# A third landing tile for the weights' double words, and fewer tile shapes: one attention + spectral + FFN kernel

## The chip, the cores and the metric

The kernel runs on one core of one Trainium2 chip. The time is device microseconds of one execution, as the median of several; the profile is that of one execution, taken on the same core, and its times start at the first instruction. Engines are named as in the profile: PE is TensorE, PEld its weight loads, DVE VectorE, ACT ScalarE, POOL GpSimd, SP the engine whose queue issues every DMA here.

## The reference, cut to what matters

Eight batches, twelve heads, 448 tokens, 64 numbers a head. Queries and keys are normalized, attention gives `x` of 448 x 768 per batch; a two-dimensional Fourier transform is mixed in, and a feed-forward block (FFN) of 768 x 3072 x 768 follows. The FFN's two weight matrices come as 64-bit floats.

```
attn = softmax(scale * rmsnorm(q, g_q) @ rmsnorm(k, g_k).T) @ v
u  = x + real(fft(fft(x, axis=1), axis=2))
un = (u - mean(u)) / sqrt(var(u) + 1e-06)
out = u + relu(un @ w_ch1) @ w_ch2        # w_ch1, w_ch2: float64
```

## The kernel before, in words

**Two streams of work.** For each batch `b`, `aux(b)` yields the attention of six pairs of heads (`attention`), then the transform and the residual rows (`spectral`); `ffn(b)` yields the feed-forward block: 24 steps `up(m)`, each 18 matmuls from a piece `w1` of 768 x 128, and 36 steps `down(g, d)`, each 12 matmuls from a piece `w2` of 512 x 128 (with one `up` ahead, four `up`, six `down`, and so on). `merge` interleaves `ffn(b)` with `aux(b + 1)` by costs written in the yields and a ratio (`RATIO_FIRST` for batch 0, `RATIO` after). The first batch's `aux(0)` has no FFN beside it and runs alone, with 28 steps of `aux(1)` mixed into its end.

**Weights.** The matmuls take each weight as a rounded part and a remainder in fp32r. In batch 0 each of the 60 pieces is made from double words by `convert` (L659): a DMA brings the words as pairs of 32-bit halves into a tile `raw` (named `dbl...`, L664 to L667); ACT takes the magnitude of the high half into a tile `bits` (named `mag...`, L670) and scales the low half (L671); DVE clamps, shifts and joins (L672, L676, L680); POOL adds the low half (L684), ACT rounds (L685), POOL takes the remainder (L686); `converted` then stores both parts to device memory (L716), and later batches load them from there (L726). Fourteen of the 60 pieces are converted during `aux(0)` by `convert_some`; the other 46 while FFN 0 uses them, beside the attention of batch 1. The `dbl` tile is free again after L684, the `mag` tile after L686. There are two `dbl` tiles: `wide` gives the tag `X` 1800 words per partition, twice, and the same tag later holds the folded rows of batches 2 and up (`fold`). There are two `mag` tiles (`SLOTS["M"]`) and three weight tiles in each stream.

**A pair's rows.** `load_pair` (L214) issues four DMAs for the raw rows of queries and keys (112 partitions x 1024 words, tag `raw`, two tiles) and six for the values (128 x 512 words, tag `v`, two tiles), one pair ahead of use. `norm_pair` reads the rows and the values; in batch 0 the values go to PE as they are, and stay until `value_pair` is through.

**Order.** Tiles of one tag share a fixed number of slots: a tile waits until the tile that had its slot is read for the last time. A scheduler lays out the order of the instructions of each engine, the DMA queue on SP among them, when the program is built, and gives tiles addresses; tiles of different tags whose lives don't overlap may be given the same bytes, and then the later one waits for the earlier one's readers. At run time each engine goes through its list in order. The slots of all tags as written come to some 54,000 words (216 KB) per partition, the sum of all `bufs` times their sizes.

Of the kernel before, what the change touches and what calls it, by code (L numbers as in the profile page):

```python
# [11 lines left out]
F32 = mybir.dt.float32  # L12
F32R = mybir.dt.float32r
U32 = mybir.dt.uint32
# [5 lines left out]
B, H, S, D = 8, 12, 448, 64  # L20
DM = H * D
DFF = 4 * DM
C = 112
NC = S // C
NPAIR = H // 2
NR = DM // 128
# [63 lines left out]
def spectral_block(ctx, tc, q, k, v, g_q, g_k, w1, w2, d1, d2, out, nb=B):  # L90
# [4 lines left out]
    sb = ctx.enter_context(tc.tile_pool(name="sb", bufs=2))  # L95
# [32 lines left out]
    def behind(ins):  # L128

        others = given.get(ins.ins.engine, [])  # L130
        if starting[0] and len(others) > LAG:
            order(
                ins, others[-1 - LAG],
                mybir.DependencyClass.NoSync, mybir.DependencyReason.DATA,
            )
# [12 lines left out]
    def bank(tag, name):  # L148
        if tag == "either":
            tag = ("q", "av")[turn[0] % 2]  # L150
            turn[0] += 1
        return ps.tile([128, 512], F32, tag=tag, name=name, bufs=BANKS[tag])
# [6 lines left out]
    def wide(name, dtype=F32):  # L159
        return sb.tile([128, 1800], dtype, tag="X", name=name, bufs=2)  # L160

    def sub(o, a, b_):
        V.tensor_tensor(out=o, in0=a, in1=b_, op=ALU.subtract)
# [50 lines left out]
    def load_pair(b, p):  # L214
        if b >= nb or (b, p) in loaded:
            return
        raw = sb.tile([C, 2, 2, NC, D], F32, tag="raw", name=f"raw{b}_{p}")
        for i, src in enumerate((q, k)):
            for h in range(2):
                nc.sync.dma_start(  # L220
                    raw[:, i, h],
                    src[b, 2 * p + h].rearrange("(c t) d -> t c d", c=NC),
                )
        vt = sb.tile([128, 4, 2, D], F32, tag="v", name=f"v{b}_{p}")
        for h in range(2):
            nc.sync.dma_start(
                vt[:, :3, h],
                v[b, 2 * p + h, 64 * h : 64 * h + 384].rearrange(
                    "(j t) d -> t j d", t=128
                ),  # L230
            )
            for z in range(2):
                nc.sync.dma_start(
                    vt[64 * z : 64 * z + 64, 3, h],
                    v[b, 2 * p + h, 384 * (1 - h) : 384 * (1 - h) + 64],
                )
        loaded[b, p] = raw, vt

    def next_pair(b, p):
        return (b, p + 1) if p + 1 < NPAIR else (b + 1, 0)  # L240
# [43 lines left out]
    def plain_s(b, p):  # L284
        return b * NPAIR + p in PLAIN_SCORES
# [3 lines left out]
    def transpose_pair(b, p):  # L289

        if b >= nb or (b, p) in ready:
            return
        load_pair(b, p)
        qk, vhl = norm_pair(b, p)
        load_pair(*next_pair(b, p))
        yield 0

        if plain_s(b, p):
            T = []
            for i, tag in enumerate(("QT", "KD")):  # L300
                pt = bank(QK_BANKS[b > 0][i], f"qk{b}_{p}_{i}")
                for c in range(NC):
                    nc.tensor.transpose(
                        pt[:, c * C : (c + 1) * C],
                        qk[:, i, c].rearrange("t h d -> t (h d)"),
                        ident[:C, :C],
                    )
                t = sb.tile([128, S], F32, tag=tag, name=f"{tag}{b}_{p}")
                A.copy(t, pt[:, :S])
                T.append(t)  # L310
                yield 420
            ready[b, p] = T[0], T[1], vhl
            return

        QT = sb.tile([128, 2, S], F32R, tag="QT", name=f"QT{b}_{p}")
        KD = sb.tile([128, 2, S], F32R, tag="KD", name=f"KD{b}_{p}")
        for i in range(2):
            pt = bank(QK_BANKS[b > 0][i], f"qk{b}_{p}_{i}")
            for c in range(NC):
                nc.tensor.transpose(  # L320
                    pt[:, c * C : (c + 1) * C], qk[:, i, c].rearrange("t h d -> t (h d)"),
                    ident[:C, :C],
                )
            src = pt[:, :S]
            if i == 0:
                A.copy(QT[lo, 0], src[lo])
                A.copy(QT[hi, 1], src[hi])
                sub(QT[hi, 0], src[lo], QT[lo, 0])
                sub(QT[lo, 1], src[hi], QT[hi, 1])
            else:  # L330
                for h, sl in enumerate((lo, hi)):
                    A.copy(KD[sl, h], src[sl])
                    sub(KL[sl, h], src[sl], KD[sl, h])
                A.copy(KD[hi, 0], KD[lo, 0].bitcast(F32))
                A.copy(KD[lo, 1], KD[hi, 1].bitcast(F32))
            yield 420

        ready[b, p] = QT, KD, vhl

# [316 lines left out]
    w1w, w2w = w1.bitcast(U32), w2.bitcast(U32)  # L656
    kept1 = [dram.tile([128, 2, NR, 128], F32, name=f"w1_{m}") for m in range(NF)]
    kept2 = [dram.tile([128, NR, 2, 4, 128], F32, name=f"w2_{g}") for g in range(NG)]
    def convert(src, bits, part, name):  # L659

        _, c, f = src.shape
        raw = wide(f"dbl{name}", U32)[:, : c * f].rearrange(  # L664
            "r (c f w) -> r c f w", c=c, w=2
        )
        nc.sync.dma_start(raw.rearrange("r c f w -> r c (f w)"), src)  # L667
        low, high = raw[:, :, :, 0], raw[:, :, :, 1]
        value = bits.bitcast(F32)
        behind(nc.scalar.activation(value, high.bitcast(F32), AF.Abs))  # L670
        behind(nc.scalar.activation(low, low, AF.Copy, scale=2.0**-29))  # L671
        behind(nc.vector.tensor_scalar(  # L672
            out=value, in0=value, scalar1=MIN_HIGH, scalar2=MAX_HIGH,
            op0=ALU.max, op1=ALU.min,
        ))
        behind(nc.vector.tensor_scalar(  # L676
            out=bits, in0=bits, scalar1=5, scalar2=2,
            op0=ALU.logical_shift_left, op1=ALU.logical_shift_right,
        ))
        behind(nc.vector.scalar_tensor_tensor(  # L680
            out=bits, in0=high, scalar=0xC0000000, in1=bits,
            op0=ALU.bitwise_and, op1=ALU.bitwise_or,
        ))
        behind(nc.gpsimd.tensor_tensor(out=bits, in0=bits, in1=low, op=ALU.add))  # L684
        behind(nc.scalar.copy(part[0], value))  # L685
        behind(nc.gpsimd.tensor_tensor(  # L686
            out=part[1], in0=value, in1=part[0], op=ALU.subtract
        ))
# [46 lines left out]
            return self.parts.pop(0)  # L735

    def w1_doubles(m):
        return w1w[:, m * 256 : (m + 1) * 256].rearrange("(c r) f -> r c f", r=128)

    def w2_doubles(i):  # L740
        g, d = i // NR, i % NR
        return w2w[g * 512 : (g + 1) * 512, d * 256 : (d + 1) * 256].rearrange(
            "(f r) e -> r f e", r=128
        )

    def w2_kept(i):
        return kept2[i // NR][:, i % NR]
# [181 lines left out]

    load_gains()  # L930
    load_pair(0, 0)
    warm()
    second = aux(1)
# [20 lines left out]

# [19 lines left out]
```

## Time and profile before

| | |
|---|---|
| time, median of 3 runs | 2231.12 us (2231.12, 2231.13, 2229.54) |
| span of the profiled execution | 2227.2 us |
| PE busy | 2092.4 us, 94% |
| DVE busy | 1612.1 us, 72% |
| ACT busy | 1060.8 us, 48% |
| POOL busy | 536.6 us, 24% |
| mean granted TensorE clock | 0.970 |

The span goes from the first to the last instruction; the three runs have no spans of their own, and the median lies 3.9 us above the profiled span. Rows named `magw1e`, `dblw2e` and the like are those of the 14 early pieces, `magw` and `dblw` those of the 46 pieces that are converted during FFN 0; `w` is a weight tile. A wait "`X <- Y: a, n`" says that X's engine stood idle for `a` us, n times, until Y ended. The chain of waits is followed back from the last instruction, and its lines give start, length and what was being waited for or done.

### The profile page before, as it was taken

How to read it: one execution, taken by the hardware profiler on the slowest of the kernel's cores; microseconds unless marked ns; L12 is line 12 of the kernel's file. 1: busy time of each engine (PE TensorE's matmuls, PEld its weight loads, DVE VectorE, ACT ScalarE, POOL GpSimd, SP SyncE). 2: the span in 40 equal slices, each digit the busy share in tenths (PEclk: the TensorE clock that was granted, in tenths of full speed). 3: DMA queues.
4: the chain of work that ended last, by engine and by line, in shares of the span. 5: the costliest groups of instructions: out<-in, count | busy, mean ns of one | idle time of the engine just before them, and what ended most of it. 6: DMA issues, size and time to landing. Idle time of an engine off the chain costs nothing.

```text
span 2227.2 us, 31403 instructions
## 1 busy us (share of the span) xinstructions
PE 2092.4 (94%) x11164; PEld 1847.3 (83%) x11164; DVE 1612.1 (72%) x3083; ACT 1060.8 (48%) x2290; POOL 536.6 (24%) x322
## 2 busy tenths in 40 slices
PE   6877978779999999999999999999999999999997
PEld 3336867668999999999999999999999999998996
DVE  7897889788788587866787587867787687763122
ACT  6866766545554355524554355524554355422100
POOL 5773567644121021111211021101221022000000
PEclk8988988889999999999999999999999999999999
DMA  5555565658656675557655675558556674549665
GB/s 155 160 172 199 188 192 192 233 197 271 192 169 183 201 215 167 177 178 230 185 168 178 207 216 168 173 173 240 179 166 182 201 224 152 181 136 280 213 209 137
DMA packets 298238, 425.32 MB, mean 191 GB/s; under 512 B 186545, under 2 KB 224418, under 8 KB 298082
## 3 DMA queue, kind: packets, MB, share of 16 engines
q1 hardware_dynamic: 298082, 423.32, 61.1%
q8 instruction: 89, 1.46, 0.3%
q14 instruction: 67, 0.55, 0.1%
HBM read 363.47 MB, written 65.27 MB: 193 GB/s over the span
## 4 chain that ended last, share of the span: by engine, by line
PE 77%; DVE 10%; DMA 4%; ACT 4%; issue 2%; POOL 2%; SPq 0%; DVEq 0%; POOLq 0%; ACTq 0%
PE h L866 29%; PE o L887 27%; PE S L357 6%; PE av L443 4%; PE pt L431 4%; DMA dblw<-w 2%; PE y L546 1%; PE qk L320 1%; POOL magw L684 1%; DVE mn L113 1%; ACT P L113 1%; DMA w<-w 1%; DVE sm L113 1%; DVE eo L113 1%; PE oT L832 1%
## 5 line engine op out<-in xcount | busy, mean ns | idle before, releaser
L887 PE MATMUL o<-hs,w 128*128 128x448 f32 x3456 | 795.9, 371 | 11.5 <-DMA w<-w 4.4
L866 PE MATMUL h<-unT,w 128*128 128x448 f32 x3456 | 787.5, 373 | 7.5 <-ACT w L685 6.3
L866 PEld LDWEIGHTS h<-unT,w 128*128 128x128 f32 x3456 | 646.7, 190 | 61.3 <-ACT w L685 7.1
L887 PEld LDWEIGHTS o<-hs,w 128*128 128x128 f32 x3456 | 639.4, 189 | 68.1 <-issue 6.0
L113 ACT ACTIVATE P<-S,mn 112x448 f32<-112x448 f32 x384 | 243.3, 635 | 222.2 <-DVE mn L113 211.4
L113 DVE TENSOR_REDUCE mn<-S 112x1 f32<-112x448 f32 x384 | 233.7, 618 | 47.0 <-PE S L357 43.9
L113 POOL TENSOR_TENSOR qkn<-raw 112x1024 f32<-112x1024 f32 x47 | 90.3, 1922 | 719.7 <-PE qk L320 493.5
L113 ACT ACTIVATE hs<-h 128x448 fp32r<-128x448 f32 x192 | 104.4, 544 | 295.4 <-PE h L866 294.3
L113 DVE TENSOR_TENSOR acc<-o,acc 128x448 f32<-128x448 f32 x240 | 149.0, 621 | 109.8 <-PE o L887 108.5
L113 DVE SCALAR_TENSOR_TENSOR hs<-h,hs 128x448 fp32r<-128x448 f32 x192 | 119.2, 621 | 126.6 <-ACT hs L113 124.6
L113 ACT CAST T<-pt 128x448 fp32r<-128x448 f32 x252 | 133.0, 533 | 136.4 <-PE pt L431 134.2
L443 PE MATMUL av<-T,vhl 128*128 128x448 f32 x504 | 178.9, 387 | 13.2 <-DVE T L113 9.6
L113 DVE TENSOR_TENSOR T<-pt,T 128x448 fp32r<-128x448 f32 x252 | 154.9, 618 | 27.9 <-ACT T L113 26.2
L113 POOL TENSOR_TENSOR ss<-ss,nhalf 112x16 f32<-112x16 f32 x48 | 147.5, 3074 | 110.4 <-DVE ss L113 107.9
L113 DVE TENSOR_SCALAR P<-P,sm 112x448 f32<-112x448 f32 x336 | 164.9, 525 | 4.7
L431 PE MATMUL pt<-ident,P 112*128 112x112 f32 x1008 | 146.6, 263 | 8.2 <-ACT P L113 4.3
L357 PE MATMUL S<-KD,QT 128*112 128x448 f32 x352 | 138.8, 396 | 9.3 <-ACT P L113 4.8
L431 PEld LDWEIGHTS pt<-ident,P 112*128 112x128 f32 x1008 | 122.8, 143 | 28.6 <-ACT P L113 4.7
L113 POOL TENSOR_TENSOR rstd<-st,nhalf 112x1 f32<-112x1 f32 (+2 forms) x32 | 18.3, 572 | 494.8 <-DVE st L113 487.4
L357 PE MATMUL S<-rounded,QT 128*112 128x448 f32 x352 | 132.2, 377 | 1.7 <-DVE rounded L113 1.6
L443 PEld LDWEIGHTS av<-T,vhl 128*128 128x128 f32 x504 | 95.5, 190 | 24.7 <-DVE T L113 11.4
L113 DVE TENSOR_SCALAR sm<-sm 112x2 f32<-112x2 f32 x192 | 60.3, 314 | 59.0 <-ACT P L113 56.6
(122 smaller groups left out, 2598.8 us busy)
## 6 DMA issues: line engine op xcount, KB each, us to landing
w<-w SPq DMA_DIRECT2D x288, 512.0 KB, 4.4
w<-w SPq DMA_DIRECT2D x192, 768.0 KB, 4.6
dblw<-w SPq DMA_DIRECT2D x30, 512.0 KB, 4.3
dblw<-w SPq DMA_DIRECT2D x16, 768.0 KB, 4.4
raw<-q SPq DMA_DIRECT2D x96, 112.0 KB, 4.5
raw<-k SPq DMA_DIRECT2D x96, 112.0 KB, 3.4
v<-v SPq DMA_DIRECT2D x96, 96.0 KB, 3.5
u_dram<-u SPq DMA_DIRECT2D x24, 336.0 KB, 3.2
```

The source lines that it names most:

```text
L113: ins = emit(*args, **kwargs)
L320: nc.tensor.transpose(pt[:, c * C : (c + 1) * C], qk[:, i, c].rearrange("t h d -> t (h d)"), ident[:C, :C],)
L357: ins = nc.tensor.matmul(s_, QT[:, h, cs], K[:, h], start=step == 0, stop=step == 1)
L431: nc.tensor.transpose(pt[:, c * C : (c + 1) * C], Pc[c][:, 512 * h + j * 128 : 512 * h + (j + 1) * 128], ident[:C, :C],)
L443: nc.tensor.matmul(av[:, :S], lv, T[:, i], start=(j == 0 and i == 0), stop=False)
L546: nc.tensor.matmul(o, src[:, par, t0 : t0 + n], D1[:, ri, par, cols], start=i != 1, stop=i != 0,)
L684: behind(nc.gpsimd.tensor_tensor(out=bits, in0=bits, in1=low, op=ALU.add))
L832: nc.tensor.transpose(op[:n, j * 128 : (j + 1) * 128], accs[b][:, 3 * half + j, t0 : t0 + n], ident,)
L866: pace(nc.tensor.matmul(o, w[:, a, c], unT[c][:, z], start=n == 0, stop=n == 17))
L887: pace(nc.tensor.matmul(o, w[:, a, f], hs[4 * g + f][:, z], start=n == 0, stop=n == 11))
```

## The change

- The double words get a tag of their own, `dbl`, with three tiles of 1536 words in place of two of 1800 words under `X`. `X` stays for the folded rows of batches 2 and up.
- The two weight matrices are given in another order: each piece of 768 x 128 (or 512 x 128) lies in one stretch, by row of the tile. A row of a tile is then one run of 6 KB (or 4 KB) in device memory, where it was six (or four) runs of 1 KB.
- A pair's raw rows and values share one tile of 1536 words, with three such tiles in place of two of 1024 and two of 512.
- `QT` and `KD` are always 900 words (they were 896, and 448 for four pairs of batch 0).

No instruction of an engine is added or removed.

```diff
-        raw = sb.tile([C, 2, 2, NC, D], F32, tag="raw", name=f"raw{b}_{p}")
+        both = sb.tile([128, 1536], F32, tag="raw", name=f"raw{b}_{p}", bufs=3)
+        raw = both[:C, :1024].rearrange(
+            "t (i h c d) -> t i h c d", i=2, h=2, c=NC
+        )
...
-        vt = sb.tile([128, 4, 2, D], F32, tag="v", name=f"v{b}_{p}")
+        vt = both[:, 1024:].rearrange("t (j h d) -> t j h d", j=4, h=2)
...
-                t = sb.tile([128, S], F32, tag=tag, name=f"{tag}{b}_{p}")
+                t = sb.tile([128, 900], F32, tag=tag, name=f"{tag}{b}_{p}")[:, :S]
...
-        QT = sb.tile([128, 2, S], F32R, tag="QT", name=f"QT{b}_{p}")
-        KD = sb.tile([128, 2, S], F32R, tag="KD", name=f"KD{b}_{p}")
+        QT = sb.tile([128, 900], F32R, tag="QT", name=f"QT{b}_{p}")[
+            :, : 2 * S
+        ].rearrange("r (h t) -> r h t", h=2)
...
-        raw = wide(f"dbl{name}", U32)[:, : c * f].rearrange(
-            "r (c f w) -> r c f w", c=c, w=2
-        )
+        raw = sb.tile([128, 1536], U32, tag="dbl", name=f"dbl{name}", bufs=3)[
+            :, : c * f
+        ].rearrange("r (c f w) -> r c f w", c=c, w=2)
...
     def w1_doubles(m):
-        return w1w[:, m * 256 : (m + 1) * 256].rearrange("(c r) f -> r c f", r=128)
+        return w1w[m]
...
-        g, d = i // NR, i % NR
-        return w2w[g * 512 : (g + 1) * 512, d * 256 : (d + 1) * 256].rearrange(
-            "(f r) e -> r f e", r=128
-        )
+        return w2w[i // NR, i % NR]
...
-        "w1": moe_w_ch1.view(np.uint64), "w2": moe_w_ch2.view(np.uint64),
+        "w1": words(moe_w_ch1.reshape(NR, 128, DFF // 128, 128).transpose(2, 1, 0, 3)),
+        "w2": words(
+            moe_w_ch2.reshape(DFF // 512, 4, 128, NR, 128).transpose(0, 3, 2, 1, 4)
+        ),
```

More of the change, by code (lines that the diff above doesn't have):

```diff
@@ L313, in transpose_pair @@
             return
-        QT = sb.tile([128, 2, S], F32R, tag="QT", name=f"QT{b}_{p}")
-        KD = sb.tile([128, 2, S], F32R, tag="KD", name=f"KD{b}_{p}")
+        QT = sb.tile([128, 900], F32R, tag="QT", name=f"QT{b}_{p}")[
+            :, : 2 * S
+        ].rearrange("r (h t) -> r h t", h=2)
+        KD = sb.tile([128, 900], F32R, tag="KD", name=f"KD{b}_{p}")[
+            :, : 2 * S
+        ].rearrange("r (h t) -> r h t", h=2)
         for i in range(2):
@@ L956, with words @@
     d1, d2 = dft_consts()
+    def words(w):
+        return np.ascontiguousarray(w).view(np.uint64)
     nc = bacc.Bacc("TRN2", target_bir_lowering=False, num_devices=1)
```

## The prediction

> **What bounds the kernel now.** I read the page's slices first, then busy time by stretch, then the chain of waits and the waits of the one stretch that is not full.
>
> ```profile
> PE   6877978779999999999999999999999999999997
> DVE  7897889788788587866787587867787687763122
> ```
> ```profile
> 739.47 5.11 PE y L546 x48
> ...
> 988.27 5.11 PE y L546 x48
> ```
> ```profile
> 537.00:788.00 251.00, 251.00 (x1400) 230.36 (x1400) 185.03 (x379) 114.16 (x254) 39.09 (x22) 1.00 0.62 190
> ```
> ```profile
> 251.00:537.00 286.00, 224.56 (x1083) 192.98 (x1082) 251.26 (x402) 177.95 (x337) 170.06 (x107) 0.87 0.63 215
> ```
>
> In the chain the same matmuls of two batches lie 248.8 us apart. The columns of the two stretches are the length and the busy time of PE, PEld, DVE, ACT and POOL, then clock and DMA. From slice 10 on PE is full: a batch takes 249 us, at a clock of 1.00, and DVE has a quarter of its time free. Nothing done to DMAs or DVE there can bring time. In 251 to 537, where most of the pieces are converted, PE stands idle for 61.4 of 286 us, its clock is at 0.87, and DVE is busy for 251.26 us, 88%. DVE is idle for 34.7 us; that is about what the stretch can lose without DVE itself doing less. Whatever is saved ahead of 537 moves all that follows.
>
> Chain of waits, the same stretch, then waits by engine:
>
> ```profile
> by line: DMA dblw<-w 14.5%; issue 10.3%; POOL magw L684 8.8%; DVE magw L680 6.4%; DVE magw L672 3.9%; DVE eo L113 3.8%; DVE magw L676 3.6%; PE h L866 3.3%; DVE mn L113 2.9%; PE o L887 2.8%; POOL w L686 2.7%; ACT magw L670 2.5%; DVE sd L113
> ...
> 253.66 4.17 DMA dblw<-w
> ...
> 490.84 5.26 DMA dblw<-w
> ```
> ```profile
> DVE magw L672 <- ACT magw L670: 16.1, 16, 2.3
> ACT magw L670 <- DMA dblw<-w: 26.6, 16, 3.8
> ACT dblw L671 <- DMA dblw<-w: 11.5, 10, 2.6
> SPq L667 <- POOL magw L684: 93.7, 34, 7.4
> ```
>
> Nine loads of double words lie on the chain in this stretch, the first and the last shown; together they are 41.6 us, 14.5% of it. ACT stands idle for them for 38.1 us (26.6 + 11.5), and DVE behind ACT for 16.1 us, the largest wait DVE has there. The SP queue shows why: its loads wait for POOL L684, the last reader of the tile before. One turn, by the timeline:
>
> ```profile
> 463.52 2.18 POOL L684 TENSOR_TENSOR magw<-magw,dblw 128x768 uint32<-128x768 uint32 x1 [1.97 <-DVE magw L680]
> 465.73 0.37 SPq L667 DMA_DIRECT2D dblw<-w  x1
> 466.64 1.91 POOL L686 TENSOR_TENSOR w<-magw,w 128x768 fp32r<-128x768 f32 x1 [0.94 <-ACT w L685]
> 470.24 0.93 ACT L670 ACTIVATE magw<-dblw 128x768 f32<-128x768 f32 x1 [3.68 <-DMA dblw<-w]
> ```
>
> L684 ends at 465.70, the load into its tile is issued at 465.73, and ACT can begin at 470.24, idle for 3.68 us. With two tiles the load is a link of the loop; with three it is issued one conversion earlier.
>
> **The change part by part.** *The third tile.* It lets a load go after L684 of the conversion three back. By the rows below the 46 conversions lie 7.6 us apart on average (their L684 from 189.9 to 531.7), and a load lands in 4.3 or 4.4 us:
>
> ```profile
> L684 POOL TENSOR_TENSOR magw<-magw,dblw x46: 1275/1345/4289, 189.9 to 531.7; 128x512 uint32<-128x512 uint32 x30, 128x768 uint32<-128x768 uint32 x16
> ```
> ```profile
> w<-w SPq DMA_DIRECT2D x288, 512.0 KB, 4.4
> w<-w SPq DMA_DIRECT2D x192, 768.0 KB, 4.6
> dblw<-w SPq DMA_DIRECT2D x30, 512.0 KB, 4.3
> dblw<-w SPq DMA_DIRECT2D x16, 768.0 KB, 4.4
> ```
>
> So the data are there when ACT asks, and the 38.1 us of ACT's waits and the 41.6 us of the chain go. What is late next? First the `mag` tiles, of which there are still two: L670 needs L686 of the conversion two back. In the turn above that ended at 468.55, so L670 could start 1.69 us earlier, not 3.68. I paired each of the 16 waits of L670 with that L686, the smaller of wait and gap counted; the first and the last pair:
>
> ```profile
> 250.26 1.53 POOL L686 TENSOR_TENSOR w<-magw,w 128x512 fp32r<-128x512 f32 x1 [1.92 <-ACT w L685]
> 252.80 0.91 ACT L670 ACTIVATE magw<-dblw 128x768 f32<-128x768 f32 x1 [2.18 <-DMA dblw<-w]
> ...
> 521.41 2.70 POOL L686 TENSOR_TENSOR w<-magw,w 128x512 fp32r<-128x512 f32 x2
> ...
> 528.01 0.68 ACT L670 ACTIVATE magw<-dblw 128x512 f32<-128x512 f32 x1 [0.33 <-DMA dblw<-w]
> ```
>
> They give 1.01 (252.80 less 251.79) and 0.33, and all 16 together 20.2 us. Second, DVE: it can only give back what it stood idle for behind these loads, 16.1 us. The least of the three bounds (41.6, 20.2, 16.1) is DVE's, and DVE is the fullest engine, so I take 16.1. It would put DVE at 251.26 of 269.9 us, 93%; the fullest it gets in any stretch I asked for is 61.20 of 66:
>
> ```profile
> 310.00:376.00 66.00, 50.28 (x244) 43.23 (x243) 61.20 (x96) 46.44 (x89) 45.22 (x26) 0.82 0.59 195
> ```
>
> That is 92.7%, which on 251.26 us of work would give 271 us and 15 us of gain: 16 is about the most that the rows bear out. Bounds: 0, where something else takes the place, and 34.7, where DVE is never idle. Over the whole run the same wait has one more occurrence, before 198:
>
> ```profile
> DVE magw L672 <- ACT magw L670: 18.3, 17, 2.3
> ```
>
> That is the 2.2 us of the early stretch; I take it too, with bounds of 0 and 7.1 (two more loads on the chain there, 3.60 and 3.51):
>
> ```profile
> 164.91 3.60 DMA dblw<-w
> ...
> 188.49 3.51 DMA dblw<-w
> ```
>
> *The layout by pieces.* Rows of 4 or 6 KB in place of 1 KB. The stored pieces, `w`, already lie in such rows, and land in 4.4 and 4.6 us where the double words take 4.3 and 4.4: I take 0. Bounds: 1 us less a load, which would be the nine of the chain, but they are covered by the third tile; nothing more.
>
> *One tile for rows and values, three of them.* It moves ten DMA issues a pair, none added. The loads of a pair wait for all readers of the pair three back, rows and values, where they waited for the pair two back; every reader is done earlier than now. On SP the load of rows is at times ahead of a load of words, and both wait:
>
> ```profile
> 284.29 1.28 POOL L684 TENSOR_TENSOR magw<-magw,dblw 128x512 uint32<-128x512 uint32 x1 [1.62 <-DVE magw L680]
> ...
> 287.56 0.88 SPq L220 DMA_DIRECT2D raw<-q  x2
> 288.53 0.44 SPq L667 DMA_DIRECT2D dblw<-w  x1
> ```
>
> The tile for that load was free at 285.57; it went at 288.53, 2.9 us late, behind rows that had waited for DVE. The third tile hides this already, so I count 0, bounds 0 and the 2.9. After 537 PE is full, and earlier rows bring nothing. *The 900 words* change no instruction: 0, but for the addresses (below).
>
> Sum: 16.1 + 2.2 = 18.3 us off the profiled span of 2227.2, giving 2208.9. The median of the runs shown lies 3.9 us above that span, so 2212.8, rounded to 2213. The later batches, the start and the tail are unchanged in it.
>
> **The rivals.** *DVE and POOL get in each other's way, no change.* In the stretch DVE's simple operations are far from their shortest:
>
> ```profile
> L672 DVE TENSOR_SCALAR magw<-magw x46: 405/522/1376, 185.2 to 528.9; 128x512 f32<-128x512 f32 x30, 128x768 f32<-128x768 f32 x16
> L676 DVE TENSOR_SCALAR magw<-magw x46: 399/430/2572, 187.8 to 529.9; 128x512 uint32<-128x512 uint32 x30, 128x768 uint32<-128x768 uint32 x16
> L680 DVE SCALAR_TENSOR_TENSOR magw<-dblw,magw x46: 675/942/2525, 188.8 to 530.8; 128x512 uint32<-128x512 uint32 x30, 128x768 uint32<-128x768 uint32 x16
> ```
> ```profile
> 431.17 1.30 POOL L684 TENSOR_TENSOR magw<-magw,dblw 128x512 uint32<-128x512 uint32 x1 [3.46 <-DVE magw L680]
> 431.31 1.71 DVE L680 SCALAR_TENSOR_TENSOR magw<-dblw,magw 128x512 uint32<-128x512 uint32 x1
> ```
>
> L680 at 431.31 starts while POOL works until 432.47, and ends at 433.02, 0.55 us after it: it seems to have waited for POOL. With less idle time the two meet more often. A collision costs L680 up to 1.85 us (2525 less 675 ns); if one more conversion in five met one, 9 x 1.85 = 17 us would go and the time be about 2230, no change. Against it: each piece brings the same POOL work as before, and 18 us over 340 makes the work only some 5% denser. The Trainium skill, "SBUF — State Buffer", section "SBUF: two separate sides", says that DVE (in a two-port mode, or with two inputs in SBUF) and GpSimd take a shared port pair as an exclusive lock, the loser blocked for the whole instruction. By it each further meeting would cost a wait, and the time would be this rival's; the row of 431.31 agrees with the rule.
>
> *More than I count.* DVE's idle time all goes: 34.7 us in place of 16.1, so 2231.1 less 34.7, 2196; with the early loads 2189. For it: the chain shows 41.6 us of loads. Against it: the two `mag` tiles.
>
> *Slower: tiles that share bytes.* Tiles of words and rows have 12,816 words per partition where they had 6,672 (3 x 1536 twice and 2 x 1800, against 2 x 1800, 2 x 1024 and 2 x 512). More of the other tiles must then lie on one another's bytes, and a tile that is loaded onto bytes in use waits. The place is a weight load late for PE in the full stretch, where one such wait stands now:
>
> ```profile
> 1478.64 5.19 DMA w<-w
> ```
>
> One in each of batches 1 to 6 would cost 6 x 5.19 = 31 us, net of 18.3 a time of 2244; from four such waits on (20.8) the kernel is slower. For it: PE has no idle time there to hide one. Against it: words and folded rows are not needed in the same stretch, and a scheduler that picks addresses can choose old ones. The Trainium skill, the same page, section "SBUF size: 192, 224, or 256?", gives about 208 KiB per partition; the sum of all slots as written was 216 KB already, so by that page some bytes are shared before the change too.
>
> **How the numbers follow.** The likeliest, DVE-bound case has 0.62, its own range 2200 to 2224 (gains of 7 to 31 us); more than that 0.11; no change 0.10; slower 0.17. Within 0.2% is within 4.5 us of 2231.1, about what the measurement can tell from no change. Faster 0.73, same 0.10, slower 0.17. The range reaches from 2190, the larger gain, into the slower case up to 2238; outside lie the rest of it and a gain beyond DVE's idle time.
>
> **What would show it.** Right: loads of double words are issued well before ACT asks, ACT's waits for them fall from 38 to a few us, and the chain has at most one or two of them; L670 waits for L686 instead; PE is full from about 519 on and not from 537; DVE's share in that stretch is near 93%; the batches after it take 249 us as now. Wrong: L672, L676 and L680 have longer means (POOL); PE idle after 537 behind weight loads or rows (bytes); or the order in which the engines' lists were laid out differs so much that the attention of batch 0 ahead of 198 is no longer the same.

## The result: 0.9% slower, and the profile after

The changed kernel takes 2247.86 us (median of 5; 2244.26 to 2259.56) where the kernel before takes 2231.12: a ratio of 1.0089 [1.0068, 1.0110]. Forecast were 2213 us, 18 us faster; it is 17 us slower. The profiled execution has a span of 2242.4 us (2227.2 before), at a mean clock of 0.965 (0.970).

The slices of the page after, PE and DVE, and in its chain the `y` matmuls of batches 2 to 6 (start, length):

```profile
PE   7876977769999999999999999999999999999997
DVE  7787799978688577876888577866788587753122
```
```profile
755.64 4.22 PE y L553 x40
1005.43 4.22 PE y L553 x40
1254.60 4.22 PE y L553 x40
1503.68 4.22 PE y L553 x40
1752.92 4.22 PE y L553 x40
```

PE is full from slice 10 on as before, and the batches after the conversions lie 249 to 250 us apart as before. The loss lies ahead of that. Where, the first matmul of FFN 0 tells (timeline of before, then of after):

```profile
194.56 0.74 PE L866 MATMUL h<-unT,w 128*128 128x448 f32 x1 [0.38 <-DVE magw L672]
```
```profile
209.20 0.74 PE L870 MATMUL h<-unT,w 128*128 128x448 f32 x1
```

It starts 14.6 us late. From there to the end of `y` of batch 2 both kernels take nearly the same: 744.58 less 194.56 is 550.0 us before, 759.86 less 209.20 is 550.7 after. To the end of the last `y` it is 1239.4 and 1240.4. So nearly the whole loss arises in the attention of batch 0, beside which only 14 of the 60 pieces are converted, and the stretch at which the change aims gave nothing. Its conversions do end sooner, 335.1 us after the first FFN matmul in place of 340.7, but PE isn't idle for less time up to there (64.1 us, before 61.4), so `y` of batch 2 doesn't come sooner.

**Batch 0.** The waits of after in 0 to 200, first those of the DMA queue, then two of the engines; behind them the queue's two waits for rows and values before:

```profile
SPq L223 <- PE av L421: 10.5, 5, 2.9
```
```profile
POOL qkn L113 <- DMA raw<-k: 14.8, 3, 6.2
DVE mn L113 <- PE S L361: 11.3, 5, 6.0
```
```profile
SPq L220 <- POOL qkn L113: 16.6, 6, 4.6
SPq L226 <- PE av L414: 12.3, 5, 4.5
```

Before, the raw rows (L220) waited for POOL's normalization, early in a pair's life, and only the values (L226) for PE's last value matmul (`av`, L414). After, the rows (L223) wait for that matmul (L421), because they share a tile with the values that it reads. The rows then land when POOL already stands. One such place, in the chain of after from 50 to 62 and in its timeline:

```profile
53.07 0.89 PE av L421 x2
...
54.72 0.95 SPq L223
55.67 0.05 issue
55.72 1.19 SPq L223
56.90 0.04 issue
56.95 3.51 DMA raw<-k
```
```profile
60.62 2.16 POOL L113 TENSOR_TENSOR qkn<-raw 112x1024 f32<-112x1024 f32 x1 [5.02 <-DMA raw<-k]
```

Value matmul, issue, transfer: a chain from the tail of one pair to the head of the pair three on. In the kernel before the same POOL instruction starts at 53.14:

```profile
53.14 1.89 POOL L113 TENSOR_TENSOR qkn<-raw 112x1024 f32<-112x1024 f32 x1
```

It is 7.5 us later, of which 0.6 were there at POOL's instruction before it (43.84 after 43.23). In batch 0 a pair is being loaded while one is normalized, one is in the scores and one in the values: four, and the change has three tiles.

PE's granted clock is lower there as well. Each line gives the stretch up to the first FFN matmul, its length twice, the busy time of PE, PEld, DVE, ACT and POOL, then clock, DMA share and GB/s: before, after, and the kernel before with nothing but the layout changed:

```profile
0.00:194.56 194.56, 138.89 (x552) 70.26 (x552) 163.68 (x278) 135.47 (x296) 120.63 (x74) 0.88 0.52 157
```
```profile
0.00:209.20 209.20, 156.82 (x553) 78.05 (x553) 164.05 (x279) 137.40 (x297) 116.63 (x74) 0.79 0.52 150
```
```profile
0.00:198.64 198.64, 148.86 (x552) 74.03 (x553) 160.10 (x279) 135.81 (x296) 119.35 (x74) 0.80 0.51 154
```

The same matmuls take PE 17.9 us longer after the change. A rival is therefore that the clock and not the rows made the loss. Against it: with the layout alone the clock is 0.80 and FFN 0 starts at 198.6, 4 us late and not 14.6. How the 14.6 us divide between waits and clock was not separated.

**The conversions.** The waits of after in 200 to 555, then of its DMA queue:

```profile
ACT dblw L678 <- DMA dblw<-w: 19.2, 15, 5.0
DVE magw L679 <- ACT magw L677: 15.7, 13, 2.7
ACT magw L677 <- POOL w L693: 11.1, 11, 2.3
```
```profile
SPq L674 <- POOL magw L691: 110.4, 40, 8.5
```

ACT's 26.6 us in front of the magnitude (L677, was L670) are gone. Its waits for loads fell from 38.1 to 19.2 us, half and not "a few", and all of them stand in front of the scaling of the low half (L678, was L671: 11.5 before), which needs no `mag` tile. In front of the magnitude ACT now waits for POOL's subtraction (L693), the last reader of the `mag` tile. DVE still stands for 15.7 us behind L677: it was 16.1. The wait that the sum was made of changed what lies behind it and kept its size. DVE is busy for 250.70 of 286 us in 266 to 552, 88% as before and not the 93% of the forecast.

### The profile page after: what moved, and what is told of

The parts are those of the page before. It is cut to its first block, busy times and chain, and to the rows that moved or that the text cites. A ratio compares the mean times of both kernels' runs of the same rounds, so it can differ in the third digit from the quotient of the medians.

```text
span 2242.4 us, 31331 instructions
## 1 busy us (share of the span) xinstructions
PE 2106.6 (94%) x11164; PEld 1852.2 (83%) x11164; DVE 1611.9 (72%) x3083; ACT 1062.6 (47%) x2290; POOL 536.4 (24%) x322
## 4 chain that ended last, share of the span: by engine, by line
PE 77%; DVE 11%; DMA 4%; ACT 3%; issue 2%; POOL 2%; SPq 0%; DVEq 0%; POOLq 0%; ACTq 0%
PE h L870 28%; PE o L891 26%; PE S L364 6%; PE av L450 4%; PE pt L438 4%; DMA w<-w 2%; PE y L553 1%; DVE eo L113 1%; PE qk L327 1%; DVE magw L687 1%; PE av L417 1%; DMA dblw<-w 1%; PE oT L836 1%; DVE mn L113 1%; ACT P L113 1%
## 5 line engine op out<-in xcount | busy, mean ns | idle before, releaser
L870 PE MATMUL h<-unT,w 128*128 128x448 f32 x3456 | 779.8, 371 | 19.2 <-ACT w L692 16.4
L113 POOL TENSOR_TENSOR rstd<-st,nhalf 112x1 f32<-112x1 f32 (+2 forms) x32 | 18.4, 576 | 494.8 <-DVE st L113 491.9
L450 PEld LDWEIGHTS av<-T,vhl 128*128 128x128 f32 x504 | 94.8, 190 | 27.8 <-DVE T L113 17.8
```

The lines of the kernel that those rows point to most:

```text
L113: ins = emit(*args, **kwargs)
L450: nc.tensor.matmul(av[:, :S], lv, T[:, i], start=(j == 0 and i == 0), stop=False)
L870: pace(nc.tensor.matmul(o, w[:, a, c], unT[c][:, z], start=n == 0, stop=n == 17))
```

## The experiments

**R**, the theory: the rows' load waits for the last value matmul of the pair three back, in batch 0, and this costs the 15 to 19 us; the third tile brings little. **P**, a rival: DVE and POOL meet more often, and DVE's clamps and shifts (L679, L683) get longer. **M**, another: the `mag` tiles hold the third tile's gain back. A short table of all runs comes first. "First h" is the first FFN matmul, "last conversion" the end of the last POOL subtraction of the 46, "last y" the end of the last `y` matmul, each in the one profile of the kernel, in us. A ratio is to runs of the kernel before that were taken beside that kernel, so it can differ a little from the quotient of the times shown.

| kernel | dbl tiles | rows, values | time | ratio to before | first h | last conversion | last y |
|---|---|---|---|---|---|---|---|
| before | 2 | apart | 2231.1 | | 194.6 | 535.2 | 1984.0 |
| after | 3 | shared | 2247.9 | 1.0089 [1.0068, 1.0110] | 209.2 | 544.3 | 2000.3 |
| layout_only | 2 | apart | 2231.2 | 0.9994 [0.9985, 1.0003] | 198.6 | 539.5 | 1988.4 |
| third_undone | 2 | shared | 2249.4 | 1.0077 [1.0061, 1.0092] | 206.7 | 549.5 | 2001.6 |
| rows_undone | 3 | apart | 2228.9 | 0.9979 [0.9969, 0.9989] | 194.4 | 530.6 | 1982.1 |
| rows_undone_dbl2 | 2 | apart | 2226.7 | 0.9978 [0.9969, 0.9987] | 198.0 | 534.8 | 1984.4 |
| rows4_dbl2 | 2 | shared, 4 | 2243.9 | 1.0060 [1.0047, 1.0072] | 196.7 | 543.9 | 1997.6 |
| mag3 | 3 | shared | 2239.3 | 1.0040 [1.0022, 1.0058] | 214.7 | 532.1 | 1996.2 |
| rows_undone_mag3 | 3 | apart | 2232.9 | 1.0008 [0.9999, 1.0017] | 199.1 | 533.2 | 1989.2 |
| own_values_900 | 3 | shared from batch 1 on | 2223.1 | 0.9966 [0.9952, 0.9979] | 193.0 | 527.5 | 1980.1 |
| own_values_900_dbl2 | 2 | the same | 2236.3 | 1.0023 [1.0014, 1.0032] | 197.4 | 538.7 | 1991.1 |
| no_pool_add | 3 | apart | 2187.0 | 0.9800 [0.9785, 0.9815] | 189.9 | 491.2 | 1946.0 |
| no_pool_add_dbl2 | 2 | apart | 2195.4 | 0.9840 [0.9827, 0.9854] | 190.2 | 498.4 | 1951.5 |
| pool_extra_512 | 2 | apart | 2254.3 | 1.0104 [1.0090, 1.0118] | 208.6 | 562.9 | 2010.9 |
| rows_undone_r46 | 3 | apart | 2232.4 | 1.0004 [0.9995, 1.0013] | 199.3 | 539.3 | 1988.5 |
| rows_undone_dbl2_r46 | 2 | apart | 2237.1 | 1.0031 [1.0017, 1.0046] | 194.7 | 545.6 | 1989.3 |
| own_values_900_r46 | 3 | shared from batch 1 on | 2225.6 | 0.9979 [0.9970, 0.9989] | 193.3 | 529.6 | 1983.3 |
| own_values_900_dbl2_r46 | 2 | the same | 2244.2 | 1.0060 [1.0043, 1.0078] | 195.4 | 548.7 | 2000.4 |
| no_loads | 3 | apart | 2221.5 | 0.9953 [0.9938, 0.9968] | 196.4 | 528.8 | 1979.1 |
| before_r46 | 2 | apart | 2241.8 | 1.0048 [1.0029, 1.0066] | 199.5 | 553.3 | 1998.4 |

The kernel before with the third tile alone, or with the shared tile alone, wasn't run; rows_undone and third_undone are the nearest to them.

**The layout alone** (the kernel before, weights by pieces):

```diff
-        return w1w[:, m * 256 : (m + 1) * 256].rearrange("(c r) f -> r c f", r=128)
+        return w1w[m]
```

> The kernel before with the weights laid out by pieces and nothing else. All theories: a load of double words lands in 4.2 to 4.8 us in both layouts, so 2231, within 5 us of before. A gain over 8 us would mean that the rows of 1 KB cost something that the landing times don't show.

Measured: 2231.15, no change. Its page has the loads at

```profile
dblw<-w SPq DMA_DIRECT2D x30, 512.0 KB, 3.8
dblw<-w SPq DMA_DIRECT2D x16, 768.0 KB, 4.3
```

against 4.3 and 4.4 us before, and nothing of it in the time. The smaller loads land sooner than the 4.2 to 4.8 us that were expected, but that isn't the layout's doing for certain: the kernel before in another order (before_r46) has 3.6 and 4.4 us with rows of 1 KB.

**Rows and values apart again, the third tile kept:**

```diff
-        both = sb.tile([128, 1536], F32, tag="raw", name=f"raw{b}_{p}", bufs=3)
-        raw = both[:C, :1024].rearrange(
+        raw = sb.tile([128, 1024], F32, tag="raw", name=f"raw{b}_{p}", bufs=2)[
...
-        vt = both[:, 1024:].rearrange("t (j h d) -> t j h d", j=4, h=2)
+        vt = sb.tile([128, 900], F32, tag="v", name=f"v{b}_{p}", bufs=2)[
```

> The changed kernel with raw rows and values in tiles of their own again, two of each as before (the values' tiles 900 words, of which 512 are used); third tile of double words, layout and 900 words stay. Theory R (rows): the 15 us lost ahead of the first FFN matmul come from the rows, which in batch 0 now wait until the values of the pair three back are through with PE; so the first FFN matmul falls from 209 to 193 to 197, POOL's and DVE's waits for raw rows there fall from about 15 to under 4 us, and the time is 2228 to 2235 if the third tile brings nothing, 2213 if it brings what was predicted. Rival S (start): the third tile is what slows batch 0, as early loads and the scaling of low halves are put ahead of other work; then the first FFN matmul stays near 209 and the time near 2247.

Measured: 2228.93, 18.9 us below the changed kernel; the first FFN matmul is back at 194.4, and POOL's normalization no longer stands for the rows (14.8 us in the changed kernel). The queue's waits in 0 to 200 are those of before:

```profile
SPq L222 <- POOL qkn L113: 17.0, 6, 4.6
SPq L230 <- PE av L422: 12.6, 5, 4.7
```

R stands: the granted clock up to the first FFN matmul is back at 0.88 with it. What is left, the third tile and the rest, is worth 2 us here.

**The third tile taken away, the rest kept** (`bufs=2` for `dbl`):

> The changed kernel with two tiles of double words, all else as changed. Theory R: the first FFN matmul stays at 205 to 213, and the stretch from it to the last conversion is as long as with three (342 to 346 us) since the two tiles of magnitudes bound it, so the time is 2243 to 2253; ACT's first read of a piece (the magnitude) waits for its load again, 25 us or so. Rival S: the first FFN matmul falls to 194 to 198 and the time to 2231. Theory of the prediction: 18 us more than the changed kernel, 2265.

Measured: 2249.35, 1.5 us above the changed kernel, with the first FFN matmul at 206.7. The tile that was to bring 18 brings next to nothing beside the shared rows. Two details of the expectation failed: the conversions take 342.8 us from the first FFN matmul, not as long as with three (335.1), and ACT's wait for loads in front of the magnitude is 13.7 us, not 25.

**Four shared tiles** (`bufs=4` for `raw`, 2 for `dbl`):

> The changed kernel with four shared tiles of rows and values in place of three, and two tiles of double words in place of three. Theory R, made exact: in batch 0 a shared tile is held from its load until the value matmuls of its pair are through, and with one pair loading, one ahead, one in its scores and one in its values that takes four; so with four the first FFN matmul comes back to 193 to 198, no load of query rows waits for PE's value matmuls ahead of 200, and the time is 2228 to 2235. Rival T: it is the sharing itself (ten loads into one tile, or the other addresses) and not the number; then the first FFN matmul stays at 205 to 210 and the time at 2245 to 2252.

Measured: the first FFN matmul is back, at 196.7, and the time isn't: 2243.88. POOL's wait for the rows falls from 14.8 to 2.1 us. So R is right about the place, but its forecast of the time is missed, and so is the one that no load of rows would wait for the value matmuls ahead of 200:

```profile
SPq L223 <- PE av L421: 9.3, 4, 4.3
```

The queue waits nearly as long as in the changed kernel (10.5 us); what went is that POOL stood for what it brought. The conversions end at 543.9, 347.2 us after the first matmul (337 to 354 in the others with two `dbl` and two `mag` tiles and POOL's work as it was), and the later batches are 4 us longer, with weight loads in the chain. The chain by line in 560 to 1010, this kernel and then before:

```profile
by line: PE h L870 34.5%; PE o L891 33.3%; PE S L364 7.6%; PE av L450 6.6%; PE pt L438 6.2%; PE y L553 2.4%; PE qk L327 1.7%; DMA w<-w 1.4%; PE av L455 1.1%; PE rem L398 1.0%; PE oT L836 0.7%; DVE eo L113 0.7%; PE ab L626 0.7%; PE un L782 0
```
```profile
by line: PE o L887 36.0%; PE h L866 34.5%; PE S L357 7.6%; PE av L443 6.6%; PE pt L431 6.2%; PE y L546 2.3%; PE qk L320 1.9%; PE av L448 1.1%; PE ab L619 1.0%; PE rem L391 0.9%; PE x L578 0.9%; PE oT L832 0.7%; PE un L778 0.5%
```

`DMA w<-w` has 1.4% there and isn't listed before. That alone doesn't account for the 4 us: in the changed kernel it has 2.1% of the same stretch, and its later batches are only 1.0 us longer. Its last `y` ends 13.6 us after that of the kernel before: 2.1 arise by the first FFN matmul, 7.3 from there to the end of `y` of batch 2, and 4.2 behind it. The cause of the last two stays open.

**A tile of their own for the values of batch 0 only,** shared tiles from batch 1 on, and the same with two `dbl` tiles:

```diff
-        vt = both[:, 1024:].rearrange("t (j h d) -> t j h d", j=4, h=2)
+        vt = (
+            sb.tile([128, 900], F32, tag="v", name=f"v{b}_{p}", bufs=2)[:, :512]
+            if plain(b, p)
+            else both[:, 1024:]
+        ).rearrange("t (j h d) -> t j h d", j=4, h=2)
```

> The changed kernel, but in batch 0 (the plain pairs) a pair's values have a tile of their own (two such tiles); in the later batches rows and values share a tile as in the changed kernel; three tiles for the double words. Theory R (the loss is the raw rows' load waiting for the last value matmul of the pair three back, in batch 0 alone): that wait is gone ahead of the first feed-forward matmul, which starts at 194 to 199 us (209.2 in the changed kernel, 194.4 with rows and values undone everywhere), from there to the end of y of batch 2 takes 548 to 552 us, and the time is 2228 to 2236 us. Rival W (a shared tile also costs in the later batches, where its loads wait longer and the kept weights' loads queue behind them): the first feed-forward matmul is as early, but from there to the end of y of batch 2 it takes over 555 us, or from there on over 1242, and the time is 2238 to 2245 us.

> As the run with own values in batch 0, but with two tiles for the double words instead of three: the one difference of the pair is the third tile. The prediction's sum held it at 16.1 + 2.2 us: then this run is 12 to 20 us slower than the one with three. Theory N (behind the loads the loop over the magnitude tiles and VectorE's and POOL's work stand next, so that the wait only changes its name): within 4 us of the one with three.

Measured: 2223.13 with three `dbl` tiles, the best of all that keep the computation whole: 8 us below the kernel before and 24.7 below the changed one, by values in tiles of their own in batch 0. The first FFN matmul is at 193.0 and the queue's waits for rows in 0 to 200 are short:

```profile
SPq L223 <- POOL qkn L113: 9.7, 4, 3.9
SPq L233 <- PE av L425: 4.7, 2, 3.1
```

This confirms R and its place a second time, though the time is below R's range of 2228 to 2236; W, a cost of sharing in the later batches, isn't seen here (547.3 us to the end of `y` of batch 2, 1239.8 from there on). But with two `dbl` tiles it is 2236.29: here the third tile is worth 13.2 us, and N is wrong.

**A third `mag` tile,** in the changed kernel, and with rows and values apart, three `dbl` tiles in both:

```diff
-    SLOTS = {"P": 8, "PT": 6, "M": 2, "unT": 6, "h": 6}
+    SLOTS = {"P": 8, "PT": 6, "M": 3, "unT": 6, "h": 6}
```

> The changed kernel with three tiles of magnitudes in place of two. Theory M (magnitudes): the third tile of double words only moved the wait, from the load to the magnitude tile two back (L677 starts within 0.1 us of the end of L693 two back in 20 of 46 conversions); with three the conversion stretch falls by 10 to 20 us, so 2228 to 2238. Rival D: DVE, at 88%, and the order of ACT's list bound the stretch whatever the tiles; then 2244 to 2252, no change to the changed kernel, and DVE stays at 88% there.

> Rows and values in tiles of their own, three tiles of double words, three of magnitudes. Theory M: the gain of the third magnitude tile adds to that of the rows: 2216 to 2224, with the first FFN matmul near 194. Theory P (port): DVE's idle time in the conversion stretch falls further, but its clamps and shifts take longer than the 67 us that they take in all with two magnitude tiles, 75 us or more, so that only some 9 of 18 us are kept. Rival D: no more than rows_undone, 2226 to 2231.

Measured: 2239.25 in the first, 8.6 us below the changed kernel although its first FFN matmul is at 214.7: the conversions end 12.2 us earlier, and their stretch falls by 17.8 us. The time is just above M's range (2228 to 2238) and below D's; DVE is busy for 268.81 of 286 us (228 to 514), 94% and not the 88% of D. In the second it is 2232.93, 4.0 us above its partner with two `mag` tiles (rows_undone, 2228.93) and above both ranges that were given. So M holds in one arrangement and not in the other. What speaks against more is seen in both: DVE's wait behind ACT falls (15.7 to 2.3 us, and 8.8 to 5.4), and DVE's own instructions take longer. Clamps and shifts of the 46, mag3 in 195 to 560, then the kernel before in 185 to 575:

```profile
L683 DVE TENSOR_SCALAR magw<-magw 128x512 uint32<-128x512 uint32 (+1 forms) x46 | 42.7, 934 | 0.5
L679 DVE TENSOR_SCALAR magw<-magw 128x512 f32<-128x512 f32 (+1 forms) x46 | 36.7, 800 | 2.6 <-ACT magw L677 2.3
```
```profile
L676 DVE TENSOR_SCALAR magw<-magw 128x512 uint32<-128x512 uint32 (+1 forms) x46 | 30.7, 668 | 0.9
L672 DVE TENSOR_SCALAR magw<-magw 128x512 f32<-128x512 f32 (+1 forms) x46 | 27.1, 589 | 18.6 <-ACT magw L670 18.3
```

79.4 us of busy time where it was 57.8, for the same instructions, and 16.0 us less of idle time (18.6 to 2.6). In the second it is 76.8 us where its partner has 69.4. That goes with P: DVE got more work out of the same instructions than the wait had been long.

**Two `dbl` tiles with rows and values apart:**

> Rows and values in tiles of their own and two tiles of double words: of the change only the layout, the 900 words and another size for the word tiles are left. All theories: 2229 to 2234, first FFN matmul at 193 to 197, as before; DVE's clamps and shifts in the conversion stretch take 54 to 59 us in all. Other than that: the 900 words or the addresses have a part in it.

Measured: 2226.65 against 2228.93 with three, a ratio to before of 0.9978 against 0.9979. Here the third tile is worth nothing. DVE's waits behind ACT and its clamps and shifts show where its gain went; two tiles, then three, in 185 to 575:

```profile
DVE magw L680 <- ACT magw L678: 18.4, 18, 2.4
```
```profile
DVE magw L680 <- ACT magw L678: 8.8, 10, 2.5
```

The third tile takes 9.6 us off the wait, and the clamps and shifts take 69.4 us in place of 60.8. All three forecasts were missed by a little: the time (2229 to 2234), the first FFN matmul (198.0; 193 to 197) and the clamps and shifts (59.5 us by the count of the expectation, which leaves out one conversion; 54 to 59). So the 900 words, the tiles' other sizes or the order that came of them are worth 4 to 5 us against the kernel before, since the layout alone is worth nothing; which of them was not tried.

**POOL's work.** POOL's addition of the low bits left out (with three and with two `dbl` tiles), and a POOL instruction added to each conversion:

```diff
-        behind(nc.gpsimd.tensor_tensor(out=bits, in0=bits, in1=low, op=ALU.add))
```
```diff
+        behind(nc.gpsimd.tensor_tensor(
+            out=scratch, in0=scratch, in1=scratch, op=ALU.mult
+        ))
```

> rows_undone without POOL's addition of the low half to the magnitude (one of POOL's two instructions a conversion is left out, and with it the low bits of the weights). Theory P: with half of POOL's conversion work gone, DVE's clamps and shifts in the stretch fall from 67 us in all to under 56, also though the conversions come closer together, and the scaling of P from a mean of 805 to under 700 ns; the time is 2208 to 2220. Rival: their length has nothing to do with POOL, they stay at 65 us or more, and what time is gained (up to 8 us) comes from the shorter loop.

> The kernel with rows and values undone, without POOL's addition of the low bits (left out: the low bits of the weights; its time before, with three double-word tiles, was 2187.0 us), now with two double-word tiles. It asks if the third tile is worth something once POOL's addition is out of the loop. Theory N (a loop over the magnitude tile, of which POOL's addition was the longest part, covers the loads): with that part gone the loads end the waits again, and two tiles are 5 to 18 us slower than three, 2192 to 2205 us; ScalarE's waits for loads, 27.1 us with three, rise to 35 us or more. Rival (VectorE's and POOL's work alone sets the pace, whatever the loads do): within 3 us of 2187.

> The kernel with rows and values undone and two double-word tiles (2226.7 us), and behind each conversion's subtraction POOL multiplies one 128x512 scratch tile by itself in place: 48 more instructions of some 1.3 us, 62 us of POOL's time by the row of its other 128x512 instructions, whose result nothing reads. In the conversions' stretch POOL is busy about 200 of 345 us, so that they would fit. Theory P (what POOL does slows VectorE's clamps and shifts beside it, and lengthens the way of the magnitude tile): clamps and shifts rise from 59.5 us by 10 or more, and the time rises by 12 to 40 us, to 2239 to 2267 us. Rival (POOL has the time to spare, and the 42 us that its addition was worth was the addition's place in each conversion's chain): clamps and shifts within 4 us of 59.5 and the time at most 6 us longer.

Measured: without the addition 2187.0, 41.9 us less, far more than was expected. Clamps and shifts of all 46 conversions are down from 69.4 to 56.1 us, but the scaling of P has a mean of 738 ns, not under 700. With two `dbl` tiles and no addition it is 2195.4: the third tile is worth 8.4 there, within N's 5 to 18. N's reason isn't borne out: ACT's waits for loads should have risen to 35 us or more with two tiles, and they are 22.6 us in 185 to 520, where they are 28.8 with three. The added multiplication costs 27.6 us (2254.29 against 2226.65), within P's 12 to 40. There are 60 of them, one for each piece and not 48; they depend on nothing, and the scheduler put 34 ahead of the first FFN matmul, which is 10.6 us later. Between that matmul and the last conversion it is 354.3 us in place of 336.9. Clamps and shifts rise by 6.5 us, from 60.8 to

```profile
L682 DVE TENSOR_SCALAR magw<-magw 128x512 f32<-128x512 f32 (+1 forms) x46 | 36.3, 789 | 15.5 <-ACT magw L680 15.2
L686 DVE TENSOR_SCALAR magw<-magw 128x512 uint32<-128x512 uint32 (+1 forms) x46 | 31.0, 675 | 0.6
```

less than the 10 that P asked for. So POOL, busy for 58% of the conversions' stretch without the multiplications (196.97 of 338 us), has no time to spare: in these two trials a microsecond of its work cost about 0.4 of time (68.8 us of multiplications for 27.6; 93.5 us of additions, the busy time of all 60 in rows_undone, for 41.9). The addition is also a link of each conversion's chain, which the multiplication is not. DVE's longer clamps and shifts are less than a third of either (6.5 and 13.3 us); the rest was not split further.

**The same resources in another order.** The scheduler builds another order for each of these kernels. To see what the order alone is worth, the share of batch 1's attention that is mixed into FFN 0 was moved by one hundredth, in five kernels:

```diff
-RATIO_FIRST = 0.45
+RATIO_FIRST = 0.46
```

> Rows and values undone, three double-word tiles, and the share of batch 1's attention that is mixed into the first feed-forward block changed from 0.45 to 0.46. No resource changes; the built order of the instructions does, by some 1500 lines on TensorE and 290 on the DMA queue. With its partner below it asks if what the third tile was worth in the four pairs so far (two tiles minus three: -2.3 us with rows and values undone, 1.5 in the changed kernel, 13.2 with own values in batch 0, 8.4 without POOL's addition) belongs to those resources or to the order that each build happened to get. Theory O (the order): this run lies up to 8 us from 2228.9 to either side, and three tiles are worth another sum here, by 4 us or more. Theory S (the resources): within 3 us of 2228.9.

> The partner with two double-word tiles, share 0.46. Theory S (with the rows' tiles apart the third tile is worth nothing, whatever the order): this run minus its partner lies between -5 and 1 us, and this run within 3 us of 2226.7. Theory O (the order of each build decides by several us): the difference lies outside -6 to 2 us.

> Own values in batch 0, three double-word tiles, share 0.46 in place of 0.45. Theory S (this arrangement is the fastest for its resources: three tiles for the rows in the later batches keep the DMA queue from standing, and so the third double-word tile comes to its worth): within 3 us of 2223.1. Theory O: 2224 to 2236 us, back with the other arrangements.

> The partner with two double-word tiles, share 0.46. Theory S (a third tile is worth 13 us in this arrangement): this run minus its partner is 9 to 17 us. Theory O (the 13.2 us were mostly the two builds' orders): the difference is under 7 us, of either sign.

> The kernel before, with the share of batch 1's attention that is mixed into the first feed-forward block at 0.46 in place of 0.45: another built order, the same resources. The two-tile kernels lost 10.5 and 8.0 us by that step and the three-tile ones 3.5 and 2.5. Theory D (two tiles are the more sensitive to the order): 5 to 12 us slower, 2236 to 2243 us. Rival (those steps are chance of each build): within 4 us of 2231, or faster.

Measured: all five are slower, those with three `dbl` tiles by 3.5 (rows apart) and 2.5 us (own values), those with two by 10.5, 8.0 and 10.7 (before). Three tiles minus two come to 4.7 and 18.7 us at 0.46. With rows apart that is O's side (it was -2.3 at 0.45). With own values it is nearer to S (13.2 and 18.7, above S's 9 to 17), and far from O's "under 7". D's range is met: in these five kernels two tiles are the more sensitive, and part of the 2231 of the kernel before is its order. The order alone also moves the clamps and shifts: 57.8 us before, 66.8 in before_r46, with the same resources. So of the rises and falls above only the large ones, 18 us with a third `mag` tile in the changed kernel and 13 without the addition, say something of P.

**No loads at all** (the first three `dbl` tiles are used again by all later conversions):

> Rows and values undone (2228.9 us), three double-word tiles that are loaded once by the first three conversions and then used again by all others: 57 of the 60 loads of double words are left out (the output is not that of the weights), each conversion still waits until POOL's addition of the one three back has read the tile. It bounds what any number of landing tiles could bring. Theory T (with three tiles the loads are nearly out of the way, and what is left is VectorE, POOL and the magnitude tile): from the first feed-forward matmul to the last conversion's end 328 to 338 us (336.2 with loads; 334 to 340 in the five builds with three tiles, 337 to 353 in those with two), time 2218 to 2231. Rival L (the loads still hold the loop with three tiles; ScalarE waits 19.3 us for them there): under 325 us, time under 2217.

Measured: 2221.53, 7.4 us below the kernel with loads; from the first FFN matmul to the last conversion 332.4 us, where it was 336.2. T stands: in this arrangement and order no deeper buffer could bring more than about 7.4 beyond three tiles, or 5.1 beyond two (2226.65). Its waits in 195 to 535 show what the rest is, three of the longest:

```profile
POOL magw L700 <- DVE magw L696: 68.7, 36, 7.9
ACT w L701 <- POOL magw L700: 30.5, 17, 8.1
ACT magw L686 <- POOL w L702: 16.4, 19, 3.5
```

POOL waits for DVE, ACT for POOL, and the magnitude for the `mag` tile; no transfer of double words is left to wait for.

## Why the prediction was wrong, step by step

- **One tile for rows and values: the step that failed.** "Every reader is done earlier than now" was put at 0, with bounds of 0 and 2.9. Three back in place of two back is later in turns, but the reader had changed as well: the rows wait for the values' last reader, which in batch 0 is PE at the end of the pair. The queue's wait before, `SPq L226 <- PE av L414`, had it on show, and the prediction read the queue's waits only in the conversions' stretch. So the rows landed when POOL already stood for them, 14.8 us in all, and FFN 0 started 14.6 us late. Undone, it gives back 18.9 us (rows apart) or 24.7 (own values in batch 0).
- **The third tile, 16.1 + 2.2: the term mis-sized, in the changed kernel to next to nothing.** There it measured 1.5 us. Over the six pairs that differ in nothing else it is worth 1.5, -2.3, 13.2, 8.4, 4.7 and 18.7 us, 7.4 in the mean; the last conversion ends 5.3, 4.2, 11.2, 7.2, 6.2 and 19.1 us earlier, 8.9 in the mean, always earlier. The two smallest of these differences, 1.5 and -2.3, lie within the spread of the runs. The sum took DVE's idle time behind the loads as the gain. In the changed kernel that idle time is still there (15.7 after 16.1): the `mag` tiles came next, as the prediction said, and were counted pair by pair against the old times only. With rows apart half of it went (18.4 to 8.8 us), and DVE's clamps and shifts grew by 8.6. A run without loads would have bounded the term: with rows apart it is 5.1 us below two tiles.
- **The layout, 0: right.** 2231.15. **The 900 words, 0:** not tried alone. Together with the layout and the tiles' other sizes they are in rows_undone_dbl2, which is 4.5 us below the kernel before; that is within what another order alone has moved.
- **The rival "DVE and POOL get in each other's way": seen, not the cause of the loss.** Clamps and shifts rose from 57.8 to 61.3 us in the changed kernel, less than the order alone moves them (66.8 in before_r46); with a third `mag` tile they take 79.4. The rule of the Trainium skill, "SBUF — State Buffer", section "SBUF: two separate sides" (DVE, in a two-port mode or with two inputs in SBUF, and GpSimd share a port pair, and one stands while the other holds it), would make instructions longer in this way. These runs agree in the sums (79.4 us, and 56.1 without POOL's addition), but no single meeting was followed.
- **The rival "slower, tiles that share bytes": right sign, not its mechanism.** Weight loads do stand in the chain of the later batches now (2.1% of 560 to 1010), but these batches lengthened by 1.0 us in all (1240.4 against 1239.4), not by 20 or more.
- **"The order ahead of 198 is no longer the same"** was named last among what would make it wrong. The start of FFN 0 did move, but by the wait for rows, with the clock lower beside it, and not by the order alone: 206.7 to 214.7 in the three kernels with three shared tiles in batch 0, 189.9 to 199.5 in all others but the one with POOL's added work.

Not settled: why tiles shared from batch 1 on help with three `dbl` tiles (2223.1 against 2228.9 apart; 2225.6 against 2232.4 at 0.46) and hurt with two (2236.3 against 2226.7; 2244.2 against 2237.1). It holds in two orders, so it is more than one draw; no run took it apart.

## What to carry to other kernels

Before two tiles are merged into one, write down the last reader of each and in which stage it reads: the merged tile has the longer life, and everything that is loaded into it waits for that reader. A wait that is removed is worth only what the next one leaves, and here also what the longer instructions beside it leave, so take the suspect out altogether once (here: no loads) before counting on its idle time. Where a scheduler orders the lists, a change of a few microseconds has to be tried in more than one order: one hundredth in a mixing ratio moved these kernels by 2.5 to 10.7 us.

## What the hardware showed that was not expected

- POOL's work was dear although POOL was idle for over 40% of the stretch: 60 additions left out (93.5 us of POOL) brought 41.9 us, and 60 multiplications on a tile that nobody reads (68.8 us, 34 of them ahead of FFN 0) cost 27.6.
- The same DVE clamps and shifts took between 54 us (no POOL addition, two `dbl` tiles) and 79 us (a third `mag` tile) in all, with no change of shape; another order of the kernel before took them from 57.8 to 66.8.
- Runs of 4 and 6 KB in place of 1 KB brought no time (2231.15 after 2231.12 us). The loads landed in 3.8 and 4.3 us where they had taken 4.3 and 4.4, but with the old layout in another order they took 3.6 and 4.4.
- The granted clock up to the first FFN matmul lay between 0.78 (mag3) and 0.88 (before) over these kernels, for the same matmuls: PE took 158.0 us for them at the one and 138.9 at the other.
